# Funnel attention into a routed feed-forward, one core: small PSUM results moved to ScalarE, transposes moved ahead of the folds, fetched rows used one half later

## The chip, the cores and the metric

The kernel runs on one core of a Trainium2 chip. A core has five engines with queues of their own: TensorE (PE in the profile; its weight loads are PEld), VectorE (DVE), ScalarE (ACT), GpSimd (POOL) and SyncE (SP), which here only issues DMAs. Each engine takes its instructions strictly in the order of its queue; an instruction that waits on a semaphore holds everything behind it on that engine. Time is device time in microseconds (us) of one execution. All times below are us unless marked ns.

## The reference

```python
# q, k, v: (8 batches, 8 heads, 1152, 64) float32
q_pool = q.reshape(B, H, S // 2, 2, D).mean(axis=3)
scores = np.matmul(q_pool, k.transpose(0, 1, 3, 2)) / np.sqrt(D)
attn = softmax(scores)                      # with + 1e-09 in the divisor
x = np.matmul(attn, v)                      # -> (8, 576, 512), heads side by side
# mixture of depths, per batch:
s = x[b] @ w_gate                           # one score a token
top = 128 tokens with the highest s
ye = np.maximum(x[b, top] @ w1, 0) @ w2     # w1: 512x1024, w2: 1024x512
out[b] = x[b]; out[b, top] += sigmoid(s[top])[:, None] * ye
```

## The kernel before, in words

All of it is float32. The main path is the class `_Plain`; the rest of the file is a fallback that the run does not enter. The order of the work is written by hand: inside `manual_schedule()` each engine's queue has the instructions in the order in which `run` emits them. Only the constants ahead of it are placed by a scheduler.

**Pairs and halves.** Heads are taken two at a time: 8 batches by 4 pairs, 32 pairs. The 576 pooled queries of a pair are split into two halves of 288, so there are 64 halves, numbered h from 0. Pair n has the halves 2n and 2n+1. One turn of the loop in `run` does, for half h:

- odd h: `load_pair` issues the load of the pair after next on SP: four `kb`/`qb` pieces each and two of `v_sb`. `kb`, `qb` and `qp` have a single buffer, `kT` and `qT` two, `v_sb` three.
- `scores(h)` (L747, L754): nine chunks of keys; for each, two matmuls into a PSUM tile and one exponent by ScalarE into `p` (two buffers). Keys and queries lie transposed in `kT`, `qT`.
- `gated(h-2)` (L861, L863): VectorE sums `prod` over the head's dimension (`red`) and, after an odd half, scales it with `rec` into `part`. After the last pair of a batch it opens the batch's routing unit, whose first piece issues the copy of `xs` into `out`, and forms `line` and `diag` (L890, L894).
- `folded(h)` (L779, L784, L793): GpSimd adds three pairs of chunks (`acc`), VectorE reduces the rest of `p` and then `acc` with two transposing folds, and adds these up (`sum`).
- `weighted(h-1)` (L762): 18 matmuls of `p` with `v_sb`; ScalarE copies the result to `av` (L770). The scores of the next half thus stand on TensorE ahead of the weighted sums of this one.
- `drained(h-1)` (L807, L810): VectorE transposes `av` into `avb`, GpSimd multiplies it with the gate's weights (`prod`).
- even h: `prepare_pair` for the pair loaded last: GpSimd adds neighbouring queries (`qp`, L726), VectorE transposes keys (`kT`, L729) and queries (`qT`, L733). It serves the scores from half h+2 on.
- even h: `normalized` for the pair that ended with h-1: TensorE merges `sum` over partitions (L822), VectorE adds 1e-9 (`sums`, L832) and inverts (`rec`, L840), GpSimd makes `x` (L842), SP writes it to `xs` in DRAM (four DMAs, L850).
- `units`: each open routing unit goes on to its next stop, the newest unit first.

**A routing unit** of batch b begins in half 8b+9. Its stops, one in each half: the scores as a row (L905 on TensorE, `sc_row`); `columns` (L664, L668, L669), the clamp of the gate (L919) and the first rank comparisons; more comparisons; more; the last ones with the one-hot `pick` (L973); L983 with `index` and `own_gate` (L991, L993) and the fetch of the 128 chosen rows (`xe`, an indirect DMA issued by GpSimd); their transposes (L1008, L1011); W1 (L1019); W2 (L1032), the update (L1041) and the scatter to `out` (L1049). What is left of the last two batches runs behind the loop, in an order written out at the end of `run`.

**PSUM** is one pool of four tiles of two banks each; `banks()` gives out the next. Scores, weighted sums and all the small results take their tiles from it, and a tile is free again when its last reader is done.

Of the kernel before, what the change touches and what calls it, by code (L numbers as in the profile page):

```python
# [10 lines left out]
P = 128  # L11
# [3 lines left out]
F32 = mybir.dt.float32  # L15
I32 = mybir.dt.int32
AF = mybir.ActivationFunctionType
ALU = mybir.AluOpType
# [516 lines left out]
class _Plain:  # L535
# [62 lines left out]
    def constants(self):  # L598
        nc, const = self.nc, self.const
        self.ident = const.tile([P, P], F32, name="ident")  # L600
        make_identity(nc, self.ident[:, :])
        self.ones = const.tile([P, P], F32, name="ones")
        nc.gpsimd.memset(self.ones[:, :], 1.0)

        self.before = const.tile([P, P], F32, name="before")
        nc.gpsimd.memset(self.before[:, :], 1.0)
        nc.gpsimd.affine_select(
            out=self.before[:, :],
            in_=self.before[:, :],
            compare_op=ALU.is_gt,  # L610
            fill=0.0,
            base=0,
            pattern=[[-1, P]],
            channel_multiplier=1,
        )
        slot_i = self.ffn.tile([P, self.Sp], I32, name="cmp")
        nc.gpsimd.iota(slot_i[:, :], pattern=[[1, self.Sp]], base=0, channel_multiplier=0)
        self.slot_f = const.tile([P, self.Sp], F32, name="slot_f")
        nc.vector.tensor_copy(self.slot_f[:, :], slot_i[:, :])

        line_i = self.ffn.tile([1, self.QB, BLK], I32, name="diag")
        nc.gpsimd.iota(
            line_i[:, :, :], pattern=[[1, self.QB], [self.QB, BLK]], base=0, channel_multiplier=0
        )
        line_f = self.ffn.tile([1, self.Sp], F32, name="sc_row")
        nc.vector.tensor_copy(line_f[:, :], line_i.rearrange("p n i -> p (n i)"))
        self.token = const.tile([P, self.NT], F32, name="token")
        self.columns(self.token, line_f, self.banks()[:, 0, :])

        self.same = const.tile([P, BLK], F32, name="same")  # L630
        nc.vector.tensor_reduce(
            self.same[:, :],
            self.ident.rearrange("p (g j) -> p j g", j=BLK),
            AX.X,
            ALU.add,
        )

        self.merge = const.tile([P, P // BLK, BLK], F32, name="merge")
        nc.vector.tensor_copy(
            self.merge[:, :, :], self.same[:, :].unsqueeze(1).broadcast_to([P, P // BLK, BLK])  # L640
        )

        self.meta = const.tile([P, self.B, self.NT, 3], F32, name="meta")
        for b in range(self.B):
            nc.gpsimd.tensor_copy(self.meta[:, b, :, 0], self.token[:, :])
            nc.gpsimd.tensor_scalar(
                out=self.meta[:, b, :, 1],
                in0=self.token[:, :],
                scalar1=float(b * self.Sp),
                scalar2=None,  # L650
                op0=ALU.add,
            )

        self.sums = const.tile([P, self.B * self.NPAIR, self.QB], F32, name="sums")
        self.w_gate = const.tile([P, self.NPAIR, BLK], F32, name="w_gate")
        self.w1 = const.tile([P, self.ND, self.F], F32, name="w1")
        self.w2 = const.tile([P, self.NFC, self.Dm], F32, name="w2")

    def columns(self, to, line, ps):

        nc, NF = self.nc, self.NF
        for t in range(self.NT):
            rows = P if t < NF else self.TAIL
            nc.tensor.transpose(  # L664
                ps[0:rows, t : t + 1], line[0:1, t * P : t * P + rows], self.ident[0:1, 0:1]
            )
        nc.vector.memset(to[:, NF : NF + 1], 0.0)
        nc.vector.tensor_copy(to[:, 0:NF], ps[:, 0:NF])  # L668
        nc.vector.tensor_copy(to[0 : self.TAIL, NF : NF + 1], ps[0 : self.TAIL, NF : NF + 1])  # L669

    def load_gate(self):
        gate = self.w_gate_in.rearrange("(n j d) -> n j d", n=self.NPAIR, j=2)
# [144 lines left out]
    def normalized(self, pair):  # L817


        nc, hb, hp = self.nc, self.HB, pair["hp"]  # L820
        ps = self.banks()[:, 0, :]
        nc.tensor.matmul(  # L822
            ps[:, 0 : 4 * hb],
            lhsT=self.merge.rearrange("p g j -> p (g j)"),
            rhs=pair["sum"].rearrange("p s n -> p (s n)"),
            start=True,
            stop=True,
        )
        tot = self.sums[:, pair["b"] * self.NPAIR + hp, :]
        for j in range(2):  # L830
            rows = slice(j * self.D, (j + 1) * self.D)
            nc.vector.tensor_scalar(  # L832
                out=tot[rows, :].rearrange("p (s n) -> p s n", s=2),
                in0=ps[rows, 0 : 4 * hb].rearrange("p (s j n) -> p s j n", s=2, j=2)[:, :, j, :],
                scalar1=1e-9,
                scalar2=None,
                op0=ALU.add,
            )
        rec = pair["rec"] = self.small.tile([P, self.QB], F32, name="rec")
        nc.vector.reciprocal(rec[:, :], tot)  # L840
        x = self.work.tile([P, self.QB, BLK], F32, name="x")
        nc.gpsimd.tensor_tensor(  # L842
            out=x[:, :, :],
            in0=pair["avb"][:, :, :],
            in1=rec[:, :].unsqueeze(2).broadcast_to([P, self.QB, BLK]),
            op=ALU.mult,
        )
        for j, ds, rows in self.quarters():
            d0 = (2 * hp + j) * self.D
            nc.sync.dma_start(  # L850
                pair["xs"][:, d0 + ds.start : d0 + ds.stop].rearrange("(i n) d -> i n d", i=BLK),
                x[rows, :, :],
            )
# [25 lines left out]
    def routed(self, b, xs, part):  # L879


        nc, ffn, Sp, NT, NF = self.nc, self.ffn, self.Sp, self.NT, self.NF
# [6 lines left out]
        line = self.small.tile([P, self.QB], F32, name="line")  # L889
# [8 lines left out]
            op=ALU.mult,  # L898
        )
        yield  # L900
        sc_row = ffn.tile([P, 2, self.HALF], F32, name="sc_row")
        flat = diag.rearrange("p n i -> p (n i)")
        ps = self.banks()
        for s in range(2):
# [4 lines left out]
                start=True,  # L909
                stop=True,  # L910
            )
        nc.scalar.copy(sc_row[:, :, :], ps[:, :, 0 : self.HALF])
        sc_row = sc_row.rearrange("p s n -> p (s n)")
        yield True
        sc = ffn.tile([P, NT], F32, name="gate_sc")
        self.columns(sc, sc_row, self.banks()[:, 0, :])
        gate = ffn.tile([P, NT], F32, name="gate")

        nc.vector.tensor_scalar(  # L919
            out=gate[:, :], in0=sc[:, :], scalar1=-88.0, scalar2=None, op0=ALU.max  # L920
        )

# [46 lines left out]
        for s0, w in self.slots:  # L969
# [12 lines left out]
            for t, rows in tiles:  # L982
# [5 lines left out]
                    stop=(t == NT - 1),  # L988
                )
            index = ffn.tile([P, 2], I32, name="index")  # L990
            nc.vector.tensor_copy(index[0:w, :], ps[0:w, 0:2])  # L991
            own_gate = ffn.tile([P, 1], F32, name="own_gate")
            nc.vector.tensor_copy(own_gate[0:w, :], ps[0:w, 2:3])  # L993
            xe = ffn.tile([P, self.Dm], F32, name="xe")
            nc.gpsimd.indirect_dma_start(
                out=xe[0:w, :],
# [3 lines left out]
                bounds_check=Sp - 1,  # L1000
                oob_is_err=False,
            )
            yield True

            xeT = ffn.tile([P, self.ND, P], F32, name="xeT")
# [96 lines left out]
    def run(self):  # L1102
# [10 lines left out]
        for h in range(n_halves + 1):  # L1113
            if h < n_halves:
                n, s = divmod(h, 2)
                if s == 0:
                    pair = upcoming
                    if pair["hp"] == 0:
                        xs = self.dram.tile([self.Sp, self.Dm], F32, name="xs")
                        part = self.ffn.tile([P, self.NPAIR, self.QB], F32, name="part")  # L1120
                    pair.update(xs=xs, part=part)
                elif n + 2 < len(pairs):
                    loaded = self.load_pair(*pairs[n + 2])
                else:
                    loaded = None
                if h > 1:
                    next(weights, None)
                half = {"pair": pair, "s": s}
                halves.append(half)
                self.scores(half)  # L1130
                if h > 1:
                    self.gated(halves[h - 2])
                self.folded(half)
            elif h > 1:
                self.gated(halves[h - 2])
            if h > 0:
                done = halves[h - 1]
                self.weighted(done)
                self.drained(done)
            if h < n_halves and s == 0 and loaded:  # L1140
                upcoming = loaded
                self.prepare_pair(upcoming)
            if h > 0 and done["s"] == 1:
                self.normalized(done["pair"])
            if h < n_halves:
                self.units()
# [91 lines left out]
```

## Time and profile before

| | |
|---|---|
| runs | 804.01, 805.33, 806.38; median 805.33 |
| profiled execution | 803.0, its span 801.3 |
| granted TensorE clock | mean 0.993 |
| DVE / ACT / POOL busy | 541.9 / 372.7 / 422.1 |
| `xe` waited for by L1008 | 7 times, 7.3 in all |
| L754 exponents, 128x576 | 576 of 679 ns |
| L779 `acc`, 128x576 | 192 of 1416 ns |
| `kb`, `qb` loads: pieces of 144 KB | median 3.2 and 3.5 from issue to landing |

A row of a timeline gives start, duration, engine, line, operation, `out<-in`, shapes and count; in brackets stands the idle time of the engine ahead of it and who ended that. A row of windows gives the stretch, its length, the busy time and count of PE, PEld, DVE, ACT and POOL, then the granted clock, the share of the DMA engines that was busy, and GB/s. Buffer numbers are left out of names.

### The profile page before, as it was taken

How to read it: one execution, taken by the hardware profiler on the slowest of the kernel's cores; microseconds unless marked ns; L12 is line 12 of the kernel's file. 1: busy time of each engine (PE TensorE's matmuls, PEld its weight loads, DVE VectorE, ACT ScalarE, POOL GpSimd, SP SyncE). 2: the span in 40 equal slices, each digit the busy share in tenths (PEclk: the TensorE clock that was granted, in tenths of full speed). 3: DMA queues.
4: the chain of work that ended last, by engine and by line, in shares of the span. 5: the costliest groups of instructions: out<-in, count | busy, mean ns of one | idle time of the engine just before them, and what ended most of it. 6: DMA issues, size and time to landing. Idle time of an engine off the chain costs nothing.

```text
span 801.3 us, 14111 instructions
## 1 busy us (share of the span) xinstructions
PE 760.9 (95%) x5503; PEld 475.7 (59%) x5503; DVE 541.9 (68%) x888; ACT 372.7 (47%) x681; POOL 422.1 (53%) x372
## 2 busy tenths in 40 slices
PE   6999989999999999999999899998999999999896
PEld 4666546566565655657556575565755657556564
DVE  4666679964698637896288762987539876398560
ACT  5555555533555335553455444554435553355310
POOL 5666666563555636655265643665536645266320
PEclk9999999999999999999999999999999999999899
DMA  9677785567155671556725557355565555450120
GB/s 156 140 154 160 156 189 105 105 117 159 28 98 101 117 163 39 95 93 114 163 53 104 95 102 162 62 92 106 100 143 86 96 92 104 125 104 16 29 88 31
DMA packets 453643, 84.97 MB, mean 106 GB/s; under 512 B 450752, under 2 KB 450752, under 8 KB 453312
## 3 DMA queue, kind: packets, MB, share of 16 engines
q1 hardware_dynamic: 446976, 79.13, 51.8%
q0 software_dynamic: 1280, 4.20, 1.7%
q10 hardware_dynamic: 5312, 0.66, 0.5%
q8 instruction: 45, 0.74, 0.4%
q14 instruction: 30, 0.25, 0.1%
HBM read 72.42 MB, written 20.97 MB: 117 GB/s over the span
## 4 chain that ended last, share of the span: by engine, by line
PE 39%; POOL 20%; issue 18%; DVE 9%; DMA 7%; ACT 4%; SPq 3%; POOLq 0%; ACTq 0%
PE ps L747 15%; POOL acc L779 13%; PE ps L762 12%; PE ps L1019 5%; PE ps L1032 4%; POOL qp L726 4%; ACT p L754 4%; DMA xe<-xs,index 3%; DVE fold L784 2%; DMA out_dram<-xs 2%; POOL x L842 1%; POOL prod L810 1%; DVE qT L733 1%; DMA v_sb<-in_v_dram 1%; DVE part L863 1%
## 5 line engine op out<-in xcount | busy, mean ns | idle before, releaser
L754 ACT ACTIVATE p<-ps 128x576 f32<-128x576 f32 x576 | 325.8, 679 | 97.0 <-PE ps L747 48.0
L747 PE MATMUL ps<-qT,kT 64*128 64x288 f32 x2304 | 326.4, 426 | 17.9 <-ACT p L754 12.3
L762 PE MATMUL ps<-p,v_sb 128*64 128x288 f32 x2304 | 293.5, 409 | 0.0
L779 POOL TENSOR_TENSOR acc<-p 128x576 f32<-128x576 f32 x192 | 266.5, 1416 | 28.5 <-ACT p L754 28.2
L747 PEld LDWEIGHTS ps<-qT,kT 64*128 64x128 f32 x2304 | 205.1, 188 | 125.8 <-ACT p L754 71.3
L762 PEld LDWEIGHTS ps<-p,v_sb 128*64 128x64 f32 x2304 | 159.8, 137 | 125.6 <-ACT p L754 24.2
L784 DVE TRANSPOSE_TENSOR_REDUCE fold<-p 128x54 f32<-128x1728 f32 x64 | 126.1, 1970 | 78.2 <-ACT p L754 78.2
L810 POOL TENSOR_TENSOR prod<-avb,w_gate 128x288 f32<-128x288 f32 x64 | 51.0, 796 | 209.8 <-DVE avb L807 194.9
L784 DVE TRANSPOSE_TENSOR_REDUCE fold<-acc 128x54 f32<-128x1728 f32 x64 | 125.2, 1957 | 50.5 <-POOL acc L779 50.4
L770 ACT COPY av<-ps 128x288 f32<-128x288 f32 x64 | 25.5, 398 | 229.2 <-PE ps L762 229.2
L842 POOL TENSOR_TENSOR x<-avb,rec 128x576 f32<-128x576 f32 x32 | 37.0, 1157 | 44.6 <-DVE rec L840 34.4
L1019 PE MATMUL ps<-xeT,w 128*128 128x128 f32 x512 | 59.6, 276 | 0.6 <-ACT xeT L1011 0.6
L1019 PEld LDWEIGHTS ps<-xeT,w 128*128 128x128 f32 x512 | 58.0, 192 | 0.8 <-ACT xeT L1011 0.7
L1032 PE MATMUL ps<-w,hT 128*128 128x512 f32 x128 | 56.5, 593 | 0.0
L726 POOL TENSOR_TENSOR qp<-qb 128x576 f32<-128x576 f32 (+1 forms) x33 | 45.1, 1366 | 7.2 <-DMA qb<-in_q_dram 7.1
L733 DVE STREAM_TRANSPOSE qT<-qp 128x576 f32<-128x576 f32 (+1 forms) x33 | 25.1, 760 | 34.4 <-POOL qp L726 34.4
L1041 DVE SCALAR_TENSOR_TENSOR xe<-ps,own_gate,xe 128x512 f32<-128x512 f32 x8 | 6.0, 751 | 59.0 <-PE ps L1032 59.0
L1049 POOL DMA_INDIRECT out_dram<-xe,index x8 | 8.3, 1034 | 70.2 <-DMA out_dram<-xs 35.1
L729 DVE STREAM_TRANSPOSE kT<-kb 128x1152 f32<-128x1152 f32 (+1 forms) x33 | 43.0, 1302 | 3.1 <-DMA kb<-in_k_dram 3.1
L1032 PEld LDWEIGHTS ps<-w,hT 128*128 128x128 f32 x128 | 24.1, 190 | 27.0 <-issue 26.3
L861 DVE TENSOR_REDUCE red<-prod 128x9 f32<-128x288 f32 x64 | 28.0, 437 | 11.2 <-POOL prod L810 11.2
L1027 ACT ACTIVATE hT<-ps 128x512 f32<-128x512 f32 x16 | 9.6, 597 | 53.3 <-PE ps L1019 53.3
(66 smaller groups left out, 332.1 us busy)
## 6 DMA issues: line engine op xcount, KB each, us to landing
v_sb<-in_v_dram SPq DMA_DIRECT2D x64, 288.0 KB, 4.1
kb<-in_k_dram SPq DMA_DIRECT2D x124, 144.0 KB, 3.2
qb<-in_q_dram SPq DMA_DIRECT2D x124, 144.0 KB, 3.5
xs<-x SPq DMA_DIRECT2D x128, 72.0 KB, 2.2
out_dram<-xs SPq DMA_DIRECT2D x8, 1152.0 KB, 7.5
w<-in_moe_w_dram SPq DMA_DIRECT2D x8, 512.0 KB, 5.5
kb<-in_k_dram SPq DMA_DIRECT2D x8, 72.0 KB, 3.0
qb<-in_q_dram ACTq DMA_DIRECT2D x8, 72.0 KB, 3.1
```

The costliest lines, as they stand in the source:

```text
L726: nc.gpsimd.tensor_tensor(out=qp[:, qs, :], in0=pair["q"][:, qs, 0, :], in1=pair["q"][:, qs, 1, :], op=ALU.add)
L729: nc.vector.transpose(pair["kT"][:, i * nk * BLK : (i + 1) * nk * BLK], pair["k"][:, ks, :].rearrange("p n d -> p (n d)"),)
L733: nc.vector.transpose(pair["qT"][:, i * nq * BLK : (i + 1) * nq * BLK], qp[:, qs, :].rearrange("p n d -> p (n d)"),)
L747: nc.tensor.matmul(sc[:, j, 0:n], lhsT=pair["kT"][rows, c * P : (c + 1) * P], rhs=pair["qT"][rows, qs], start=True, stop=True,)
L754: nc.scalar.activation(p[:, c // G, c % G, :, :], sc[:, :, 0:n], AF.Exp, scale=self.scale)
L762: nc.tensor.matmul(av[j * self.D : (j + 1) * self.D, 0:n], lhsT=half["pair"]["v"][:, j, c, :], rhs=half["p"][:, c // G, c % G, j, :], star ...
L779: nc.gpsimd.tensor_tensor(out=acc[:, u, :], in0=units[:, 0, u, :], in1=units[:, 1, u, :], op=ALU.add)
L784: nc.vector.tensor_reduce(fold[:, a, :], of.rearrange("p u (m d) -> p (u m) d", d=BLK), AX.X, ALU.add, apply_transpose=True,)
L810: nc.gpsimd.tensor_tensor(out=pair["prod"][:, ns, :], in0=pair["avb"][:, ns, :], in1=self.w_gate[:, hp : hp + 1, :].broadcast_to([P, hb, B ...
L842: nc.gpsimd.tensor_tensor(out=x[:, :, :], in0=pair["avb"][:, :, :], in1=rec[:, :].unsqueeze(2).broadcast_to([P, self.QB, BLK]), op=ALU.mult,)
L1019: nc.tensor.matmul(pv[:, f, 0:w], lhsT=self.w1[:, c, (f0 + f) * P : (f0 + f + 1) * P], rhs=xeT[:, c, 0:w], start=(c == 0), stop=(c == self ...
L1032: nc.tensor.matmul(ps[0:w, 0 : self.Dm], lhsT=hT[:, f, 0:w], rhs=self.w2[:, f, :], start=(f == 0), stop=(f == self.NFC - 1),)
```

## The change

- `sums`, `columns`, `index` and `own_gate` are read from PSUM by ScalarE instead of VectorE. For `columns` the row of scores gets 64 zeros at its end (a GpSimd memset), so that one copy is enough. For `sums`, 1e-9 becomes the bias of an activation (`tiny`).
- The clamp of the gate goes from VectorE to GpSimd.
- One more stop lies between the fetch of the rows and their transposes; the units go on once more in the turn after the last half, ahead of its weighted sums.
- `prepare_pair` goes from behind `drained` to the front of the turn, ahead of `scores`, `gated` and `folded`; in the first turn it comes after `folded`, as there is nothing else.

```diff
-        line_f = self.ffn.tile([1, self.Sp], F32, name="sc_row")
-        nc.vector.tensor_copy(line_f[:, :], line_i.rearrange("p n i -> p (n i)"))
+        line_f = self.line_of_scores()
+        nc.vector.tensor_copy(line_f[0:1, 0 : self.Sp], line_i.rearrange("p n i -> p (n i)"))
...
+        self.tiny = const.tile([P, 1], F32, name="tiny")
+        nc.gpsimd.memset(self.tiny[:, :], 1e-9)
...
+    def line_of_scores(self):
+
+        line = self.ffn.tile([P, self.NT * P], F32, name="sc_row")
+        self.nc.gpsimd.memset(line[0:1, self.Sp :], 0.0)
+        return line
+
+    def columns(self, to, line):
+
+        nc = self.nc
+        ps = self.banks()[:, 0, 0 : self.NT]
         for t in range(self.NT):
-            rows = P if t < NF else self.TAIL
             nc.tensor.transpose(
-                ps[0:rows, t : t + 1], line[0:1, t * P : t * P + rows], self.ident[0:1, 0:1]
-            )
-        nc.vector.memset(to[:, NF : NF + 1], 0.0)
-        nc.vector.tensor_copy(to[:, 0:NF], ps[:, 0:NF])
-        nc.vector.tensor_copy(to[0 : self.TAIL, NF : NF + 1], ps[0 : self.TAIL, NF : NF + 1])
+                ps[:, t : t + 1], line[0:1, t * P : (t + 1) * P], self.ident[0:1, 0:1]
+            )
+        nc.scalar.copy(to[:, :], ps)
...
-            nc.vector.tensor_scalar(
-                out=tot[rows, :].rearrange("p (s n) -> p s n", s=2),
-                in0=ps[rows, 0 : 4 * hb].rearrange("p (s j n) -> p s j n", s=2, j=2)[:, :, j, :],
-                scalar1=1e-9,
-                scalar2=None,
-                op0=ALU.add,
+            nc.scalar.activation(
+                tot[rows, :].rearrange("p (s n) -> p s n", s=2),
+                ps[rows, 0 : 4 * hb].rearrange("p (s j n) -> p s j n", s=2, j=2)[:, :, j, :],
+                AF.Identity,
+                bias=self.tiny[rows, 0:1],
             )
...
-        nc.vector.tensor_scalar(
+        nc.gpsimd.tensor_scalar(
             out=gate[:, :], in0=sc[:, :], scalar1=-88.0, scalar2=None, op0=ALU.max
         )
...
-            nc.vector.tensor_copy(index[0:w, :], ps[0:w, 0:2])
+            nc.scalar.copy(index[0:w, :], ps[0:w, 0:2])
             own_gate = ffn.tile([P, 1], F32, name="own_gate")
-            nc.vector.tensor_copy(own_gate[0:w, :], ps[0:w, 2:3])
+            nc.scalar.copy(own_gate[0:w, :], ps[0:w, 2:3])
...
+            yield True
             yield True
...
+                if s == 0 and h > 0 and loaded:
+                    upcoming = loaded
+                    self.prepare_pair(upcoming)
                 half = {"pair": pair, "s": s}
                 halves.append(half)
                 self.scores(half)
                 if h > 1:
                     self.gated(halves[h - 2])
                 self.folded(half)
+                if h == 0 and loaded:
+                    upcoming = loaded
+                    self.prepare_pair(upcoming)
             elif h > 1:
                 self.gated(halves[h - 2])
+            if h == n_halves:
+                self.units()
             if h > 0:
                 done = halves[h - 1]
                 self.weighted(done)
                 self.drained(done)
-            if h < n_halves and s == 0 and loaded:
-                upcoming = loaded
-                self.prepare_pair(upcoming)
             if h > 0 and done["s"] == 1:
                 self.normalized(done["pair"])
```

More of the change, by code (lines that the diff above doesn't have):

```diff
@@ L624, in constants @@
         )
-        line_f = self.ffn.tile([1, self.Sp], F32, name="sc_row")
-        nc.vector.tensor_copy(line_f[:, :], line_i.rearrange("p n i -> p (n i)"))
+        line_f = self.line_of_scores()
+        nc.vector.tensor_copy(line_f[0:1, 0 : self.Sp], line_i.rearrange("p n i -> p (n i)"))
         self.token = const.tile([P, self.NT], F32, name="token")
-        self.columns(self.token, line_f, self.banks()[:, 0, :])
+        self.columns(self.token, line_f)
         self.same = const.tile([P, BLK], F32, name="same")
@@ L657, in constants @@
         self.w2 = const.tile([P, self.NFC, self.Dm], F32, name="w2")
-    def columns(self, to, line, ps):
-        nc, NF = self.nc, self.NF
+    def line_of_scores(self):
[5 more added lines that the diff above has]
+        ps = self.banks()[:, 0, 0 : self.NT]
         for t in range(self.NT):
-            rows = P if t < NF else self.TAIL
             nc.tensor.transpose(
-                ps[0:rows, t : t + 1], line[0:1, t * P : t * P + rows], self.ident[0:1, 0:1]
+                ps[:, t : t + 1], line[0:1, t * P : (t + 1) * P], self.ident[0:1, 0:1]
             )
-        nc.vector.memset(to[:, NF : NF + 1], 0.0)
-        nc.vector.tensor_copy(to[:, 0:NF], ps[:, 0:NF])
-        nc.vector.tensor_copy(to[0 : self.TAIL, NF : NF + 1], ps[0 : self.TAIL, NF : NF + 1])
+        nc.scalar.copy(to[:, :], ps)
     def load_gate(self):
@@ L900, in routed @@
         yield
-        sc_row = ffn.tile([P, 2, self.HALF], F32, name="sc_row")
+        sc_row = self.line_of_scores()
         flat = diag.rearrange("p n i -> p (n i)")
@@ L911, in routed @@
             )
-        nc.scalar.copy(sc_row[:, :, :], ps[:, :, 0 : self.HALF])
-        sc_row = sc_row.rearrange("p s n -> p (s n)")
+        nc.scalar.copy(
+            sc_row[:, 0:Sp].rearrange("p (s n) -> p s n", s=2), ps[:, :, 0 : self.HALF]
+        )
         yield True
         sc = ffn.tile([P, NT], F32, name="gate_sc")
-        self.columns(sc, sc_row, self.banks()[:, 0, :])
+        self.columns(sc, sc_row)
         gate = ffn.tile([P, NT], F32, name="gate")
-        nc.vector.tensor_scalar(
+        nc.gpsimd.tensor_scalar(
             out=gate[:, :], in0=sc[:, :], scalar1=-88.0, scalar2=None, op0=ALU.max
```

## The prediction

> **What bounds the kernel now.** I read the page first, then the waits by engine, then TensorE's timeline half by half, then one pair of heads on all engines.
>
> ```profile
> span 801.3 us, 14111 instructions
> PE 760.9 (95%) x5503; PEld 475.7 (59%) x5503; DVE 541.9 (68%) x888; ACT 372.7 (47%) x681; POOL 422.1 (53%) x372
> PE ps L747 <- ACT p L754: 12.3, 52, 0.3
> PE ps L1008 <- DMA xe<-xs,index: 7.3, 7, 1.7
> ```
>
> TensorE looks full, and its listed waits are small. But the shares hide stretched work, which the timeline shows:
>
> ```profile
> 339.77 4.63 PE L747 MATMUL ps<-qT,kT 64*128 64x288 f32 x36
> 344.33 4.59 PE L762 MATMUL ps<-p,v_sb 128*64 128x288 f32 x36
> ...
> 350.30 1.21 PE L747 MATMUL ps<-qT,kT 64*128 64x288 f32 x7
> 351.84 1.30 PE L747 MATMUL ps<-qT,kT 64*128 64x288 f32 x8 [0.32 <-ACT p L754]
> 353.34 1.30 PE L747 MATMUL ps<-qT,kT 64*128 64x288 f32 x8 [0.21 <-ACT p L754]
> ```
>
> The scores of a half take 4.57 from start to next start when all four banks turn over on ScalarE, but 4.96 where `sums` (L832) still holds one (17 halves) and 6.8 where VectorE holds two, `sums` with `columns` (8 halves) or with `index` (7). Behind a late VectorE read, two or three banks remain. Excess: 17x0.39 + 8x2.2 + 7x2.3 = 40 us, besides the 7.3 for fetched rows.
>
> Now the other engines over one pair (columns: start, duration). I number halves from 0; S(h) is the start of the scores of half h, X(h) the start of the `x` product in even half h. S(8) is 80.07 and X(8) is 99.36:
>
> ```profile
> 79.77 1.16 POOL L842 TENSOR_TENSOR x<-avb,rec 128x576 f32<-128x576 f32 x1 [1.59 <-DVE rec L840]
> 80.95 2.62 SPq L850 DMA_DIRECT2D xs<-x  x4
> 83.66 0.57 SPq L699 DMA_DIRECT2D kb<-in_k_dram  x1
> 88.64 4.14 POOL L779 TENSOR_TENSOR acc<-p 128x576 f32<-128x576 f32 x3
> 90.14 1.00 SPq L705 DMA_DIRECT2D qb<-in_q_dram  x1
> 92.82 1.98 DVE L784 TRANSPOSE_TENSOR_REDUCE fold<-acc 128x54 f32<-128x1728 f32 x1 [1.76 <-POOL acc L779]
> 95.09 0.47 DVE L807 STREAM_TRANSPOSE avb<-av 128x288 f32<-128x288 f32 x1
> 95.64 0.80 POOL L810 TENSOR_TENSOR prod<-avb,w_gate 128x288 f32<-128x288 f32 x1 [2.85 <-DVE avb L807]
> 96.40 1.40 POOL L726 TENSOR_TENSOR qp<-qb 128x576 f32<-128x576 f32 x1
> 97.83 0.78 DVE L733 STREAM_TRANSPOSE qT<-qp 128x576 f32<-128x576 f32 x1 [1.01 <-POOL qp L726]
> 98.62 0.36 DVE L832 TENSOR_SCALAR sums<-ps 64x18 f32<-64x18 f32 x2
> 99.36 1.16 POOL L842 TENSOR_TENSOR x<-avb,rec 128x576 f32<-128x576 f32 x1 [1.56 <-DVE rec L840]
> 102.64 1.21 PE L905 MATMUL ps<-diag,ones 128*128 128x288 f32 x4 [3.60 <-DVE diag L894]
> ```
>
> X comes every 19.6 us here, TensorE needs 18.9 a pair: GpSimd and VectorE run a loop nearly as long as TensorE's. The load of the pair after next stands on SP behind `xs`, so behind X. Its last `qb` is issued 10.4 after X (90.14-79.77) and lands 3.5 later (the median; 2.5 to 5.4): X+13.9. `qp` runs at X+16.6, so the load is hidden by under 3 us.
>
> **The change, part by part.**
>
> *Small PSUM reads on ScalarE.* 64 `sums`, 9 `columns`, 16 `index`/`own_gate` move from VectorE (0.12 to 0.16 each) to ScalarE. The nearest rows there are 0.21 (`gate` 128x5) and 0.40 (`av` 128x288). I take 0.21, nearest in size; two fit in the 0.68 that ScalarE idles between `av` and the first exponent (89.27+0.40 to 90.35). At 0.40 each they would delay the exponents by 0.12 in 32 halves, 4 us; a gain bound is nothing beyond the freed banks. The banks come free at once: TensorE's need falls by the 40 above. At the start the copy of `token` brings the activation table's load (1.28, now between ScalarE's DMA issues and the first exponent) forward: 0 to 1.3 sooner.
>
> *Fetched rows a half later.* Removes 7.3 of waiting. Every unit grows by a half: W1 (7.32) leaves half 8b+16 for 8b+17, W2 (6.96) goes to 8b+18. In half 8b+17 the newest unit goes first, so L905 of the next batch now stands on TensorE *ahead* of W1. Before, W1 covered the way from X through `part` and `diag` to L905. That cover goes.
>
> *Clamp on GpSimd.* VectorE loses 8x0.86, GpSimd gains 8x0.29 (the +1.0 row at L962) and nine tiny memsets of 0.1. It stands behind `x`, with `acc` of the next half behind it; that waits for exponents anyway. Nothing, at most 3.
>
> *Transposes in front of the folds.* VectorE's `kT`, `qT` and GpSimd's `qp` go ahead of `red`, the folds and `acc` of the same half. The chain `avb`, `qp`, `qT`, `sums`, `rec`, X loses 2.9 (99.36 against 96.44, where `prod` ends). But `qp` now waits for the load, and on GpSimd `acc`, `prod` and `x` are queued behind it; on VectorE the folds are queued behind `kT` and `qT`. SP's order is the same. So a loop closes: X, `xs` and load 13.9, `qp` 1.41, `acc` 4.14, then 3.62 from the end of `acc` through fold, sum, `avb`, `prod` (92.78 to 96.40) to the next X: **23.1** against 19.6. A landing at 2.5 or 5.4 makes it 22.1 or 25.0. TensorE meets it at L822, which needs `sum` of the odd half: `acc` of that half follows X, its fold and `sum` end at X+7.7 (87.42-79.77), so pairs that TensorE could do in 18.5 take 23.1 once X trails S by 20.
>
> **The sum.** TensorE alone would need, between even halves (start to next start in its timeline), 18.5 (2x4.57, 2x4.52 and L822's 0.34), 19.6 with L983 (1.1), 27.4 with xeT (0.56), L905 (1.07) and W1, 25.9 with `columns` (0.37) and W2: 91.4 a batch; today 97.7. Four loops are 92.4. To these come two hand-offs. (i) X+2.75 to L905: `rec` to `diag` end takes 3.46 (99.02 to 102.48) and now starts 0.7 before X. (ii) X cannot follow S by less than about 11.45: weighted ends at S+9.1, exponents at 5.9, last `acc` at 7.3, two folds 9.8, sum, `avb` 10.6, `prod`.
>
> First 18 halves: the queries of the third pair land at 27.26+3.5 = 30.8, and 1.41, 4.14 and 3.62 later X(2) = 40.0 (40.59 before). Seven loops: X(16) = 201.7, where it was 182.96. Then L905 at +2.75, it takes 1.07, W1 7.32: S(18) = 212.8 against 202.07. A loss of 10.7, and W2 is still to come.
>
> A batch from then on: X(16) to S(18) 11.1; to S(20) 25.9; X(20) is at S(20)+11.45 (later than two loops by 2.2); two loops 46.2. Together **94.6**, against 97.7. Five batches give X(56) = 674.7.
>
> Tail: S(58) 685.8, S(60) 711.7, S(62) 730.2, and 24.6 (two scores, three weighted sums, L822, L983, xeT) to the end of the last weighted sum: 754.8 (760.3 before). After it the path is the old one, 41.0 long (to 801.3), less about 0.3 for VectorE's copies: 795.5.
>
> The clock remains: TensorE now idles about 3.2 before each L905 (94.6-91.4), six times (8 at the first). The trace has two such idle spells. At 99.0 the clock stayed at 1.0. At 742 it did not:
>
> ```profile
> 744.00:746.00 2.00, 1.32 (x6) 1.12 (x8) 1.86 (x8) 0.00 (x0) 1.78 (x2) 0.50 0.00 0
> ```
>
> There the scores took 9.79, against 6.74 with the same banks at full clock: 3.05 dearer. One of two spells, so 6x1.5 = 9 (bounds 0 and 18). W1 is directly behind and on the loop, so nothing hides it. Span **804.5**. [...]
>
> The median of the runs stands 4.0 over this span (805.33 against 801.3): **808.5**.
>
> **Rivals.**
>
> *Four bare loops* (faster). If X(20) does not wait for W2, and the clock holds, a batch is 92.4: 795.5 - 5x2.2 = 784.5, time 788.5; with that wait but no clock loss 799.5. It decides where X trails S by under 9.3 instead of 11.45. For it: `acc` may start on early exponents. Against: `avb` needs the weighted sums of the half before. 0.20.
>
> *TensorE alone* (much faster). Loads land before `qp` asks; then 801.3 less 40, 7.3 and 5: 749, time 753. It needs a landing by about X+9.3 (18.5-1.41-4.14-3.62), where the last issue alone is at +10.4. 0.07.
>
> *Every spell drops the clock, or landings nearer 5.4.* 18 instead of 9: 817; with 0.5 more on each of 17 loops, 826. 0.18.
>
> *The banks do not come free*, as ScalarE reads too late behind `av`: the `columns` half lies on the loop, 5x2.6 more, 821. Against: halves whose reads are ScalarE's take 4.57. 0.05.
>
> **How the numbers follow.** The forecast holds 0.50, at 808.5. About 0.3% (2.4 us) is what a measurement can tell from no change, so faster is under 802.9, slower over 807.8. Of the forecast's 0.50 (clock loss 0 to 18, and 0.3 either way on each of 17 loops) 0.05 falls under 802.9, 0.08 between, 0.37 above; of the bare loops' 0.20, 0.14 under and 0.06 between. Faster 0.05+0.14+0.07 = 0.26; same 0.08+0.06 = 0.14; slower 0.37+0.18+0.05 = 0.60. The range 793 to 823 leaves out TensorE alone and the ends of the outer rivals.
>
> **What would show it.** GpSimd's `qp` waiting on DMA `qb` some 4 us per pair, X every 23 in plain pairs, X(8) near 109 and X(16) near 202; L905 waiting on `diag` in every batch, over 8 us at the first two; no scores at 6.8 except at half clock; no wait on `xe`; 0.5 clock after some L905 waits. A pair period near 19 with no wait on `qb` would prove the loop wrong; a batch of 94.6 at full clock, only the clock term.

## The result, and the profile after

The changed kernel takes 854.45 us (median of 4 runs, 851.94 to 855.65), the kernel before it on the same chip 805.86 (804.01 to 806.91): a ratio of 1.0602, interval 1.0570 to 1.0633. It is slower, as forecast, but by 49 us and not by 3: 46 above the forecast, 31 above the top of the range. The profiled execution has a span of 852.9 at a granted clock of 0.950.

The page of the changed kernel: span, TensorE's share, the clock in 40 slices, the loads' DMA queue, and the loads from issue to landing.

```profile
span 852.9 us, 14151 instructions
PE 761.1 (89%) x5503; PEld 506.7 (59%) x5503; DVE 506.4 (59%) x773; ACT 389.0 (46%) x770; POOL 427.4 (50%) x390
PEclk9899979989799997999989998999989999899999
q1 hardware_dynamic: 446976, 79.13, 64.2%
kb<-in_k_dram SPq DMA_DIRECT2D x124, 144.0 KB, 4.5
qb<-in_q_dram SPq DMA_DIRECT2D x124, 144.0 KB, 4.6
```

TensorE does the same 5503 matmuls in the same busy time, spread over 52 us more. One row was not expected: the queue that loads keys, queries and values moves the same packets and bytes as before, but its packets take 64.2% of the DMA engines' time, where the kernel before has this:

```profile
q1 hardware_dynamic: 446976, 79.13, 51.8%
```

The waits of the changed kernel (total, times, longest), then one loop of X in its timeline (start, duration, then as before; X(8) is 121.48):

```profile
POOL qp L732 <- DMA qb<-in_q_dram: 95.6, 17, 7.9
DVE kT L735 <- DMA kb<-in_k_dram: 62.2, 14, 7.8
PE ps L910 <- DVE diag L899: 56.5, 7, 9.4
```

```profile
121.48 1.16 POOL L847 TENSOR_TENSOR x<-avb,rec 128x576 f32<-128x576 f32 x1
122.67 2.62 SPq L855 DMA_DIRECT2D xs<-x  x4
124.76 2.26 PE L910 MATMUL ps<-diag,ones 128*128 128x288 f32 x4 [9.24 <-DVE diag L899]
125.38 0.57 SPq L705 DMA_DIRECT2D kb<-in_k_dram  x1
126.94 5.71 PE L753 MATMUL ps<-qT,kT 64*128 64x288 f32 x36
133.05 0.75 SPq L711 DMA_DIRECT2D qb<-in_q_dram  x1
137.57 1.39 POOL L732 TENSOR_TENSOR qp<-qb 128x576 f32<-128x576 f32 x1 [6.61 <-DMA qb<-in_q_dram]
138.93 4.14 POOL L785 TENSOR_TENSOR acc<-p 128x576 f32<-128x576 f32 x3
145.92 0.80 POOL L816 TENSOR_TENSOR prod<-avb,w_gate 128x288 f32<-128x288 f32 x1 [2.85 <-DVE avb L813]
146.67 1.16 POOL L847 TENSOR_TENSOR x<-avb,rec 128x576 f32<-128x576 f32 x1
```

This is the loop of the prediction, row by row: X, the four `xs` issues, the load behind them on SP, `qp` when the last `qb` lands (121.48 to 137.57, so X+16.1), `acc`, the next X. It takes 25.2 and not 23.1. (The change moves lines: L910 is the old L905, L753 the old L747, L732 the old L726, L1026 the old L1019.) TensorE idles 9.24 ahead of L910, and the windows behind it (columns: busy time of PE, PEld, DVE, ACT and POOL, granted clock, DMA share, GB/s) show the clock halved:

```profile
125.00:127.00 2.00, 2.00 (x6) 0.96 (x6) 1.50 (x1) 0.00 (x0) 2.00 (x2) 0.50 0.67 107
131.00:134.00 3.00, 3.00 (x26) 1.86 (x24) 0.00 (x0) 2.74 (x6) 0.00 (x0) 1.00 0.94 92
```

At full clock the scores take 4.57 nearly everywhere (4.96 in one half of each batch, behind W2 and `columns`), and only one wait for `xe` is left, of 0.3 in the tail: the gains are there too.

### The profile page after: what moved, and what is told of

It is laid out like the page before. It is cut to its first block, busy times and chain, and to the rows that moved or that the text cites. A ratio compares the mean times of both kernels' runs of the same rounds, so it can differ in the third digit from the quotient of the medians.

```text
span 852.9 us, 14151 instructions
## 1 busy us (share of the span) xinstructions
PE 761.1 (89%) x5503; PEld 506.7 (59%) x5503; DVE 506.4 (59%) x773; ACT 389.0 (46%) x770; POOL 427.4 (50%) x390
## 3 DMA queue, kind: packets, MB, share of 16 engines
q1 hardware_dynamic: 446976, 79.13, 64.2%
## 5 line engine op out<-in xcount | busy, mean ns | idle before, releaser
L760 ACT ACTIVATE p<-ps 128x576 f32<-128x576 f32 x576 | 321.2, 683 | 76.0 <-issue 48.0
L753 PE MATMUL ps<-qT,kT 64*128 64x288 f32 x2304 | 311.6, 421 | 11.9 <-DVE qT L739 9.3
L753 PEld LDWEIGHTS ps<-qT,kT 64*128 64x128 f32 x2304 | 224.4, 192 | 88.7 <-issue 22.3
L785 POOL TENSOR_TENSOR acc<-p 128x576 f32<-128x576 f32 x192 | 268.8, 1430 | 10.4 <-ACT p L760 10.1
L732 POOL TENSOR_TENSOR qp<-qb 128x576 f32<-128x576 f32 (+1 forms) x33 | 45.7, 1386 | 159.3 <-DMA qb<-in_q_dram 95.6
L910 PE MATMUL ps<-diag,ones 128*128 128x288 f32 x32 | 17.0, 683 | 56.7 <-DVE diag L899 56.5
L1026 PEld LDWEIGHTS ps<-xeT,w 128*128 128x128 f32 x512 | 65.7, 210 | 2.7 <-ACT xeT L1018 0.9
L1026 PE MATMUL ps<-xeT,w 128*128 128x128 f32 x512 | 65.4, 293 | 0.7 <-ACT xeT L1018 0.7
L910 PEld LDWEIGHTS ps<-diag,ones 128*128 128x128 f32 x32 | 8.9, 307 | 62.4 <-issue 59.9
L1039 PEld LDWEIGHTS ps<-w,hT 128*128 128x128 f32 x128 | 23.6, 190 | 26.4 <-issue 26.3
L917 ACT COPY sc_row<-ps 128x576 f32<-128x576 f32 x8 | 5.1, 640 | 70.3 <-PE ps L910 70.3
L866 DVE TENSOR_REDUCE red<-prod 128x9 f32<-128x288 f32 x64 | 27.6, 431 | 14.4 <-POOL prod L816 14.4
```

The source lines that it names most:

```text
L732: nc.gpsimd.tensor_tensor(out=qp[:, qs, :], in0=pair["q"][:, qs, 0, :], in1=pair["q"][:, qs, 1, :], op=ALU.add)
L753: nc.tensor.matmul(sc[:, j, 0:n], lhsT=pair["kT"][rows, c * P : (c + 1) * P], rhs=pair["qT"][rows, qs], start=True, stop=True,)
L760: nc.scalar.activation(p[:, c // G, c % G, :, :], sc[:, :, 0:n], AF.Exp, scale=self.scale)
L785: nc.gpsimd.tensor_tensor(out=acc[:, u, :], in0=units[:, 0, u, :], in1=units[:, 1, u, :], op=ALU.add)
L866: nc.vector.tensor_reduce(pair["red"][:, ns], pair["prod"][:, ns, :], AX.X, ALU.add)
L1026: nc.tensor.matmul(pv[:, f, 0:w], lhsT=self.w1[:, c, (f0 + f) * P : (f0 + f + 1) * P], rhs=xeT[:, c, 0:w], start=(c == 0), stop=(c == self ...
```

## The experiments

All times are medians of four runs, unless said otherwise; ratios are to the kernel before on the same chip. The kernel before took 804.7 to 805.9 beside all runs below but those of 761.78 and 829.08, on whose chip it took 809.03: where these two are compared with others, the difference by the ratios is given too. Every kernel computes all of the reference. "Front" means `prepare_pair` ahead of the folds, as changed; "back" means behind `drained`, as before.

### What made the loads slower

The built programs show one thing that the diff does not: the new `tiny`, 4 bytes a partition, moves the SBUF tiles behind it by 32 bytes, `kb`, `qb` and `v_sb` among them (`kb` from byte 57088, a multiple of 128 and of 256, to 57120). In the trace, the packets of 128 bytes on the loads' queue (keys and queries, and one in five a store of `x`, whose tile moved too) take 16.7 ns on average after the change and 12.7 before; those of 256 bytes, which only the loads of `v_sb` have, take 27.2 and 18.0.

```diff
-        self.tiny = const.tile([P, 1], F32, name="tiny")
+        self.tiny = const.tile([P, 32], F32, name="tiny")
```

> The changed kernel, with the new constant `tiny` 128 bytes wide instead of 4 (it takes 32), so that the tiles behind it in SBUF (kb, qb, v_sb, w1, w2) begin 128 bytes further instead of 32. Theory (place in SBUF): the 128-byte packets of the loads no longer straddle a boundary, take 12.7 ns again instead of 16.7, the last queries land at X+14.0 instead of X+15.8, the loop from X to X takes 23.1 instead of 25.3, L905's successor waits 3 to 4 us a batch instead of 9: time 805 to 815, about what was forecast. Rival (rhythm: the packets are slow because loads now run beside other work): nothing changes, 854, packets 16.7.

Measured: 826.02 (823.17 to 828.80), ratio 1.0259 [1.0221, 1.0297]. Page and waits of this kernel:

```profile
q1 hardware_dynamic: 446976, 79.13, 50.7%
POOL qp L732 <- DMA qb<-in_q_dram: 76.9, 17, 5.9
PE ps L910 <- DVE diag L899: 42.1, 7, 9.3
```

Packets are back at 12.7 ns; 28 of the 49 us were the 32 bytes. The time is still above what was expected, by 11, and 17.5 above the forecast. The loop still takes 23.6, so X(16) comes 4.4 later than forecast; then five batches take 98.8 each where 94.6 was said, and of these 4.2 the forecast had 1.5 as the cost of the clock.

The converse, the kernel before with an unused constant of 4 bytes in the same place:

```diff
+        self.tiny = const.tile([P, 1], F32, name="tiny")
+        nc.gpsimd.memset(self.tiny[:, :], 1e-9)
```

> The kernel before, with one unused constant of 4 bytes ahead of meta, which moves kb, qb, v_sb, w1, w2 by 32 bytes and changes nothing else. Theory (place in SBUF): packets of 128 bytes take about 16.7 ns instead of 12.7 from the first microsecond on; the first matmul of scores starts about 1 us later, the first X some 3 to 6 later; afterwards the load lands near X+15.8, still ahead of qp at X+16.6, so it stays hidden: 806 to 815. Rival (rhythm): packets 12.7, time 805.9 as before.

Measured: 809.60 (808.05 to 810.08), ratio 1.0058 [1.0036, 1.0080]; packets 16.2 ns, and on its page:

```profile
q1 hardware_dynamic: 446976, 79.13, 66.0%
```

The same slow packets cost 0.6% where `qp` still comes after the landing (X+15.5, with `qp` 0.9 to 2.8 behind it in the first plain pairs). X comes every 19.58 there as before; 2.7 of the 4.9 us are lost ahead of the first X, in the loads of the start. The 32 bytes were dear only on the loop: 28 us in the changed kernel, 4.9 in this one.

Is a multiple of 64 bytes enough, or does it take one of 128? The fastest back kernel below (759.12), with `tiny` of 64 bytes, so that `kb` starts at 64 past a multiple of 128 (one run):

> The kernel with the transposes back and the oldest unit first, tiny 64 bytes wide instead of 128: the tiles of the loads begin on a multiple of 64 that is none of 128. Theory (the boundary is 64 bytes): packets of 128 bytes take 12.7 ns, time as that kernel's own. Rival (the boundary is 128 or more): about 16 ns.

Measured: 763.77, packets 15.3 ns, q1 at 66.7% against 55.2%. A multiple of 64 was not enough. One of 256 was hardly better than one of 128: the kernel before has its load tiles at a multiple of 256 and the kernels with `tiny` of 128 bytes have them 128 past one; packets of 128 bytes take 12.7 to 12.8 in all of these, packets of 256 bytes 18.0 and 18.9 to 19.2. Other multiples were not tried.

### The transposes put back

```diff
-                if s == 0 and h > 0 and loaded:
-                    upcoming = loaded
-                    self.prepare_pair(upcoming)
...
+            if h < n_halves and s == 0 and loaded:
+                upcoming = loaded
+                self.prepare_pair(upcoming)
```

With `tiny` of 128 bytes, and with 4 as in the change:

> The changed kernel with tiny 128 bytes wide and the transposes of keys and queries put back behind the drain, where they stood before. Theory (the load is on the loop only because of the move): qp no longer waits for the load, X comes every 19 us in plain pairs, TensorE is the bound with 91.4 a batch, L905's successor waits at the first batch only: 750 to 765. Rival (the moved W1 alone brings the wait for diag; the transposes are innocent): the wait for diag stays at 3 us or more in every batch, time above 785.

> The changed kernel with the transposes put back behind the drain, tiny left at 4 bytes. Theory: packets still 16.7 ns and landings at X+15.8, with qp due at about X+16.3 they are just hidden: 755 to 772, within 10 of the aligned one; the slow packets cost much only where the load is on the loop. Rival (slow packets cost the same anywhere): as much above the aligned one as the changed kernel is above its own aligned form, 40 us or more.

Measured: 782.54 (781.68 to 784.59), ratio 0.9728 [0.9702, 0.9754], and 783.92 (783.61 to 787.66), ratio 0.9752 [0.9720, 0.9784]. The placement makes 1.4 here, less than the runs of one kernel differ by: its theory, that slow packets cost little off the loop, holds. The times expected of both (750 to 765, 755 to 772) were missed: X comes every 19.9 over the first seven loops, but a batch still takes 95.4, for a reason seen in the waits of the first kernel.

```profile
PE ps L910 <- DVE diag L899: 17.5, 7, 3.3
```

In half 8b+17 the newest unit goes first, so L910 stands ahead of W1 and waits for `diag`, with half the clock behind it (the first L910 takes 2.19, in the kernel before 1.21). The prediction named this hand-off. Its test is the order of the units:

```diff
-        for unit in self.routing[::-1]:
+        for unit in self.routing[:]:
```

With the transposes back, and in front:

> The kernel of the run with tiny widened and the transposes put back (782.5), with one more edit: in each half the oldest routing unit goes first, so that W1 stands on TensorE ahead of the next batch's diag matmuls again. Theory (what is left there is the wait for diag, 2.2 to 3.3 a batch, and the half clock behind it): no wait for diag from the second batch on, no half clock there, a batch of about 91.5 instead of 95.7: 757 to 765. Rival (something else holds the batch at 95.7, as GpSimd's and VectorE's own loop): time stays above 777.

> The changed kernel with tiny widened (826.0), transposes in front as changed, and the oldest unit first. Theory (two prices: the loop through the load, and the way from X through diag to W1, 13.6 a batch): W1 covers diag again, the loop alone remains, four times 23.7, a batch of 95 instead of 99: 797 to 808. Rival (the wait for diag is all, the loop is hidden without it): a batch near 91.5, 765 to 785.

Measured: back 759.12 (758.31 to 759.91), ratio 0.9433 [0.9399, 0.9468]; front 798.56 (794.05 to 804.30, ten runs), ratio 0.9917 [0.9883, 0.9951]. Both as expected. With W1 ahead of it, L910 of the back kernel waits once (its row is below), and a batch takes 91.6 where the prediction put TensorE's own need at 91.4. The front kernel keeps the loop: 23.7 for each of the first seven.

```profile
PE ps L910 <- DVE diag L899: 3.3, 1, 3.3
```

The half more between fetch and use, taken out of the 782.54 kernel:

```diff
             yield True
-            yield True
...
-            if h == n_halves:
-                self.units()
```

> tiny widened, transposes put back, and the extra half between fetch and transposes taken out again: what is left of the change is the small PSUM reads on ScalarE and the clamp on GpSimd. Theory (the extra half is what put diag ahead of W1): no wait for diag from the second batch on; the fetched rows are waited for by about 1 us a batch as before; banks free, so no scores over 5.0: a batch of 92 to 93, 762 to 772. Rival (the extra half was a gain in itself): slower than the kernel with the extra half, above 783.

Measured: 792.36 (792.12 to 792.66), ratio 0.9851 [0.9816, 0.9886]: a miss, the rival held. From the third batch on TensorE comes to the transposes of the rows 10.3 after L983 started, where the kernel before comes 12.5 after it, since the scores between are no longer stretched; the rows land no sooner: the wait for them is three times that of the kernel before. This kernel's waits:

```profile
PE ps L1014 <- DMA xe<-xs,index: 21.7, 8, 3.9
```

### The loop, opened where SP closes it

So far the loop had gone away only with the transposes. The prediction says that it closes through SP, where the load stands behind `xs`, and so behind X. That can be undone alone: `normalized` keeps the four `xs` issues, and the loop emits them behind the load of the next odd half (and behind the last half).

```diff
-        for j, ds, rows in self.quarters():
+        self.rows = {"x": x, "xs": pair["xs"], "hp": hp}
...
                 elif n + 2 < len(pairs):
                     loaded = self.load_pair(*pairs[n + 2])
                 else:
                     loaded = None
+                if s == 1:
+                    self.stored()
...
```

`stored` issues the same four DMAs. First in the front kernel with `tiny` of 128 bytes and the oldest unit first (798.56), then in the changed kernel itself with nothing else altered (854.45):

> The kernel of 798.6 us (transposes in front of the folds, `tiny` of 128 bytes, oldest unit first), with one thing changed: the four issues of `xs` of a pair stand on SP behind the loads of the next half and not in front of them; the transposes and `qp` stay in front of the folds. Theory (the loop closes only through SP's order: X to x to `xs` to load to `qp`): the load goes out once `qp` and kT have read the buffers, lands some 10 us later and ahead of the next `qp`, no `qp` waits for a load, X comes every 19 to 20 us in plain pairs: 757 to 770 us. Rival (the place in front of the folds costs by itself, since VectorE and GpSimd do 3.5 us there that the folds then wait for): 780 us or more with no wait of `qp` for a load.

> The changed kernel (854.5 us, `tiny` of 4 bytes, newest unit first, transposes in front) with one thing changed: the issues of `xs` stand on SP behind the loads of the next half. Theory (nearly all of the 49 us lost is the loop, and slow packets and the wait for `diag` were dear only through it): no `qp` waits for the load in plain pairs, X every 18 to 20 us, the wait for `diag` some 2 to 3 us a batch with half the clock behind it, as with the transposes put back: 775 to 790 us. Rival (the slow packets or the wait for `diag` cost by themselves): over 800 us, with L910 waiting 5 us and more for `diag` in every batch.

Measured: 754.16 (754.04 to 754.25), ratio 0.9356 [0.9334, 0.9378]; and 761.78 (761.17 to 762.90), ratio 0.9425 [0.9391, 0.9459]. Both are faster than the range expected of them, by 3 and by 13. From the second (where L910 is L918, and `diag` L907): page, waits, and the timeline of one pair.

```profile
span 759.4 us, 14194 instructions
q1 hardware_dynamic: 446976, 79.13, 67.5%
POOL qp L732 <- DMA qb<-in_q_dram: 13.0, 3, 5.9
PE ps L918 <- DVE diag L907: 2.6, 2, 2.2
```

```profile
89.92 1.40 POOL L732 TENSOR_TENSOR qp<-qb 128x576 f32<-128x576 f32 x1
90.37 0.33 SPq L705 DMA_DIRECT2D kb<-in_k_dram  x1
...
98.79 0.99 SPq L711 DMA_DIRECT2D qb<-in_q_dram  x1
99.02 1.16 POOL L847 TENSOR_TENSOR x<-avb,rec 128x576 f32<-128x576 f32 x1
```

The load now goes out while `qp` still runs, 9 us *ahead* of X. Its last `qb` is issued at 98.79, and with the 4.5 that this page gives for the median `qb` it lands at an estimated 103.3; the next `qp` runs at 108.5, behind `prod` and not behind the load. X comes every 18.0 in the first plain pairs. Packets are nearly as slow as in the changed kernel (15.6 ns against 16.7), and what they cost here cannot be much: the kernel of 754.16, with `tiny` of 128 bytes and the oldest unit first, is 8 us faster (6 by the ratios). Of the 854.45, 92.7 us (95 by the ratios) hung on the order of two groups of issues on SP.

The 775 to 790 that was expected came from the back kernels, whose L910 waits in every batch. Here the transposes and `qp` no longer stand between `avb` and X, so X and `diag` are earlier (X(16) follows S(16) by 16.1, in the 783.92 kernel by 18.6): TensorE idles 2.18 ahead of the first L918 and 0.39 ahead of the second, where the 783.92 kernel waits 17.2 in all. Against that kernel it is 22 us faster (26 by the ratios); part of it could be SP's order itself, as no back kernel with the load ahead of `xs` was run.

### The price of the small reads

`sums`, `columns`, `index` and `own_gate` back on VectorE, all else kept, in the 759.12 kernel and in the 782.54 kernel:

```diff
-        nc.scalar.copy(to[:, :], ps)
+        nc.vector.tensor_copy(to[:, :], ps)
...
-            nc.scalar.copy(index[0:w, :], ps[0:w, 0:2])
+            nc.vector.tensor_copy(index[0:w, :], ps[0:w, 0:2])
...
```

> The kernel of 759.1 us, with one thing undone: the small results in PSUM (`sums`, `gate_sc`/`token`, `index`, `own_gate`) are read by VectorE again and not by ScalarE. Theory (the prediction's 40 us of freed banks): VectorE stands behind its folds of 2 us when the small result is ready, so the bank comes free late and the scores behind it take 4.96 (behind each row sum) and 6.8 us (behind the columns) again where they now take 4.57: 790 to 805 us. Rival (the half more and the order of the units hide it, so that the reads were worth little by themselves): under 770 us.

> The kernel of 782.5 us (transposes behind `drained`, `tiny` of 128 bytes, newest unit first) with one thing undone: the small results in PSUM are read by VectorE again. Theory (the reads by VectorE are worth the 40 us of stretched scores that the prediction counted, of which the wait for `diag` and the half clock behind it, some 3.5 us a batch, are covered again): scores of 4.96 and 6.8 us again, 800 to 815 us, so 18 to 32 us for the reads alone. Rival (the reads cost as much as in the kernel of 864.5 us, where the same edit was worth 105 us): over 850 us.

Measured: 864.49 (857.13 to 869.38), ratio 1.0714 [1.0641, 1.0786], and 829.08 (825.74 to 832.14), ratio 1.0254 [1.0203, 1.0304]. With the transposes back, the reads are worth 105 us with the oldest unit first, far above what was expected, and 47 (42 by the ratios) with the newest first, above it too. The timeline of the 864.49 kernel behind W2 and the columns shows why:

```profile
212.81 0.47 PE L672 MATMUL ps<-ident,sc_row 1*128 1x1 f32 x5
213.58 0.16 DVE L675 COPY gate_sc<-ps 128x5 f32<-128x5 f32 x1
...
215.29 0.18 DVE L869 TENSOR_TENSOR part<-red,rec 128x18 f32<-128x18 f32 x1
219.85 1.33 PE L753 MATMUL ps<-qT,kT 64*128 64x288 f32 x4 [0.75 <-ACT p L760]
228.17 1.33 PE L753 MATMUL ps<-qT,kT 64*128 64x288 f32 x4 [0.75 <-ACT p L760]
230.24 1.98 DVE L790 TRANSPOSE_TENSOR_REDUCE fold<-p 128x54 f32<-128x1728 f32 x1 [14.77 <-ACT p L760]
```

Each chunk of scores waits for the exponent of the chunk just before, as if there were one tile of PSUM; the half takes 16.2, and from 217.68 on the clock is halved. Yet VectorE ended its last read of PSUM at 213.74 and idled from 215.47 on, for 14.77: no read is late. The built program tells what is held. The pool's four tiles (called banks here), A to D, in the order in which the scores of this half get them, and in the same half of the 759.12 kernel:

```text
reads on VectorE:  C C C C C C C C C
reads on ScalarE:  A D B A D B A D B
```

Which bank comes next is settled when the program is built. There the three banks that VectorE reads (the update of W2's rows, `columns`, `sums`) are passed over for the whole half, whenever the read ends on the chip; why it is built so is not shown. With the half more, three such reads fall into one half. In the 829.08 kernel this half begins on one bank too (five chunks of nine), and takes 10.4. The built program of the kernel before shows the same in small: the scores go round three banks in the halves of 4.96, and round two in those of 6.8 and 7.0. So the half more is a gain of 10 with the reads on ScalarE (792.36 to 782.54); no kernel was run with the reads on VectorE that differs in that half alone.

### All together

| | load behind `xs` | load ahead of `xs` |
|---|---|---|
| front, `tiny` 4 bytes, newest unit first | 854.45 (the change) | 761.78 |
| front, 128 bytes, newest first | 826.02 | |
| front, 128 bytes, oldest first | 798.56 | **754.16** |
| back, 4 bytes, newest first | 783.92 | |
| back, 128 bytes, newest first | 782.54 | |
| back, 128 bytes, oldest first | 759.12 | |

The best, 754.16, is 6.4% faster than the kernel before. It is the whole change with three things altered: a constant of 128 bytes, the order of the units, and the order of two groups of issues on SP. On its page TensorE is busy for 98% of the span, at a mean granted clock of 0.998:

```profile
span 752.4 us, 14200 instructions
PE 737.2 (98%) x5503; PEld 489.2 (65%) x5503; DVE 523.9 (70%) x773; ACT 387.8 (52%) x770; POOL 427.2 (57%) x390
PEclk9999999999999999999999999999999999999999
```

## Why the prediction was right, and where it was wrong

**The loop: right in mechanism, mis-sized.** "X, `xs` and load 13.9, `qp` 1.41, `acc` 4.14, then 3.62" is what the trace shows, and opening the loop took its cost away. The step that failed is its first term, the 13.9 from X to the landing of the last `qb`. It measured 14.7 to 16.9, 15.8 on average over the 29 loads behind an X, of which 5.1 after the issue: the pieces of keys and queries took 4.5 and 4.6 at the median where the page of before had 3.2 and 3.5. The reason is `tiny`, which the prediction left out of its sum altogether: "small PSUM reads" were costed by their instructions, and what the new constant does to addresses was not asked. With the tiles at a multiple of 128 again (826.02) the average is X+14.4, 4.0 after the last issue, and the loop 23.6: the remaining 0.5 is the last `qb`, which lands later than the median of all `qb` that the prediction took. That could be read before: in the kernel before the last `qb` lands 3.9 after its issue on average, not 3.5.

What this does to the sum: X(2) at 46.2 instead of 40.0, since the loads of the start are slow too; seven loops of 25.0 instead of 23.1 bring X(16) to 221.5 where 201.7 stood; two loops in each batch 50.4 instead of 46.2 (the batch from X(16)).

**The hand-off at L910: right in kind, too small in size.** From X(16) to L910 3.3 instead of 2.75. Then half the clock: L910 2.1 instead of 1.07 and W1 7.9 instead of 7.32 (start to next start), in every batch from there on and not in one of two. X(16) to S(18) is 13.2 against 11.1 without the clock, or 12.6 with its 1.5. The other terms of the batch stand: S(18) to S(20) 26.4 for 25.9, S(20) to X(20) 11.3 for 11.45. Five batches take 101.4 each for 94.6, so X(56) is at 728.4 where 674.7 was said. That is 53.7 late; the span is 48.4 over the forecast's, which has another 9 for the clock. "Idles about 3.2 before each L905" was wrong, 7.0 to 9.4 in the trace: it was worked out as batch less TensorE's need, and went up with the batch.

The 1.5 a batch for the clock came near what was measured (1.3 to 2.4 on L910 and W1 together, batch by batch) by luck. It is half of the 3.05 by which the scores at 742 were dearer, one spell of two, and most of that 3.05 is no clock: this row of the kernel before has 2.60 of waiting for VectorE's read of `sums`, where the like half at full clock waits 0.32.

```profile
744.68 6.04 PE L747 MATMUL ps<-qT,kT 64*128 64x288 f32 x28 [2.60 <-DVE sums L832]
```

**Banks: right in size, the reason not the whole of it.** From the fourth half on, the scores of the 782.54 kernel take 37 us less than those of the kernel before, where 40 was said. That the reads alone are worth 47 there is no test of the 40: that number also holds the halves on one bank, which cost more, and waits for `diag` that are covered again. On ScalarE `sums` takes 0.27, the others 0.16 to 0.17, where 0.21 was taken, and the scores stay at 4.57. "Behind a late VectorE read" fits the kernel before, where `sums` is read at 98.62, after the scores of 89.50 to 94.45; but the 864.49 kernel has a half on one bank with no late read, so what counts there is the order of banks in the built program. For the kernel before the two cannot be told apart.

**Fetched rows: right.** No wait for `xe` but 0.3 in the tail. But the 7.3 is no longer its price: in the 792.36 kernel, without the half more, the wait was 21.7, with half the clock behind some of it (mean 0.977).

**Clamp on GpSimd:** nothing in the waits; not tried alone.

**The rivals.** "TensorE alone" (753) was not what happened, but close to what the change becomes once the load no longer waits for X (761.78), with the constant and the units' order altered too (754.16). Its condition, a landing by X+9.3, could be met by moving issues: the load that lands at an estimated 103.3 does so 4.3 behind X. "Landings nearer 5.4" came closest. Its price used 0.5 a loop on 17 loops, although the text had just worked out 25.0 for a landing of 5.4: 1.9 on each of 17 is 32, which puts the rival at 840, and at 850 with all of the clock's 18. The range was cut at 823, with a bound of its own working outside it.

## What to carry to other kernels

When a consumer is moved forward, follow each load that it needs back to its issue, and ask what stands ahead of that issue on the queue: a store that waits for the pipeline's last result turns prefetching into a loop (here of 25.2 us, where TensorE alone would need 18.5 by the prediction's sum). Moving the store behind the load cost nothing that showed here. When a constant or a buffer is added, compare the addresses of the DMA destinations before and after; they are part of the change (28 of the 49 us here). A bound that the working yields for a term on the loop belongs in the range, times the number of loops.

## What the runs showed of the hardware

In these runs the time of the small packets went with the place of their tiles in SBUF. Packets of 128 bytes took 12.7 to 12.8 ns on average with the tiles at a multiple of 128 bytes, 15.3 at 64 past it (one run) and 15.6 to 16.7 at 32 past it; packets of 256 bytes, all of them loads, 18.0 at a multiple of 256, 18.9 to 19.2 at 128 past, 25.7 at 64 past and 24.4 to 27.2 at 32 past. Between the kernel before and the changed one this is 51.8% against 64.2% of the engines' time for the same bytes. Where the load was hidden it cost at most 0.6%, on the loop 28 us. Both places off a multiple of 128 were dearer; for packets of 256 bytes 128 past was nearly as cheap as the multiple of 256. Between 32 and 64 past, the runs of one place differ too much to tell. What makes a place dear is not shown.

Around L910 half the clock came in stretches of 3.41 us or two or three times that: 3.41 in the 782.54 kernel, mostly 6.83 in the 826.02 one, 6.83 or 10.24 in the changed kernel. The long ones begin while TensorE is still idle (217.90 to 228.14 in the changed kernel, with L910 at 224.73); in all three kernels the half clock ended 3.0 to 5.6 after the start of L910. In the 782.54 kernel it came with idle spells of 2.15 to 3.25 ahead of L910, in six of seven batches. What sets when it comes and how long it lasts is not shown.
